# Down products of two row groups by Strassen's scheme on slab pairs, in a spectral filter with a gated FFN

## The chip, the cores and the metric

The kernel runs on one core of one Trainium2 chip. The metric is the device time of one execution in microseconds (us); for the kernel before, the median of three runs is 199.85 us (199.35 to 199.93).

A core has five engines, each with an instruction queue of its own that runs in order: PE (TensorE, matmuls; PEld is its loading of weights), DVE (VectorE), ACT (ScalarE), POOL (GpSimd) and SP (SyncE, which here only issues DMAs). They wait for each other through semaphores. Matmuls write to PSUM, from where DVE and ACT take the results.

## The reference

```python
x = A_x                                  # 1 x 2048 x 640, bf16
xn = _layernorm(x, axis=-1)
X = rfft2(xn) * (w_r + 1j * w_i)         # over rows (2048) and columns (640)
s = irfft2(X)
g = silu((gelu(xn @ w_gate) * (xn @ w_up)) @ w_down)   # 640 -> 1536 -> 640
return x + s * g
```

Two branches read the same normalised rows: a 2-D Fourier filter (s), and a gated feed-forward network (g). The product of the two is added to x.

## The kernel before

The 2048 rows are cut into 16 slabs of 128 rows, and the slabs into four groups of four (512 rows). Everything stays in SBUF, apart from two turns through DRAM in the Fourier branch (ZDR after the transform along columns, UDR after the filter).

**The order is written out by hand.** A list `back` holds the work of the FFN in 144 steps, and a list `plan` of the same length holds what is put behind each step with `put(step, function, ...)`. At the end a loop emits step 0, then its extras, step 1, and so on. Every engine runs its instructions in this order of emission; no scheduler moves any of them. A step number is therefore a place in the queue of each engine, not a time.

The steps: 0 to 23 belong to the gate and up products of group 0, 24 to 35 to its down product. Group 1 has steps 36 to 59 for gate and up and 60 to 71 for down; group 2 has 72 to 95 and 96 to 107; group 3 has 108 to 131 and 132 to 143.

**The FFN.** In `ffn_half(g, t, k)` five matmuls of 512 columns make one of the twelve 128-wide pieces t of the gate product (k = 0, bank psg) or of the up product (k = 1, bank psu) for 512 rows. ACT takes the gate out with gelu (`ge`, L807), DVE multiplies the up product by it (L809) into `uT[t]`, which lies transposed: the inner dimension on the partitions, rows along the free axis. `down_third(g, j, q)` then makes a third of the down product of slab j: per slab two halves of 320 columns, each a chain of twelve matmuls over t (L828), so 24 matmuls per slab and 96 per group. When a half is complete, the gate of the output is formed: silu by ACT for groups 0 and 3, and for groups 1 and 2 a tanh on ACT (L836) and a multiply-add on DVE (L837). The banks psg and psu have two buffers each.

**The rows.** `slab_T(n, 2)` transposes a normalised slab by a DMA transpose on SP's queue (L539) into `xnT`, the moving operand of gate and up. For slabs 8 to 11 it is put at steps 34, 37, 40, 43; for slabs 12 to 15 at steps 65, 68, 71, 74.

**The Fourier branch.** For each slab `slab_S1` (five small matmuls) and `slab_D` (six) transform the folded rows: ACT copies the result to a tile `zd` (L591, six buffers), and SP stores it in two DMAs to ZDR (L594). The last is slab 15's `slab_D`, put at step 60. At the same step `load_B2` issues ten DMAs that read ZDR back the other way round into B2 (L612); they wait for the stores. Then come eleven bursts: `s2_in` (matmuls px, L638; copy by ACT, L646; two multiplications with the filter's weights on DVE, L650) and `s2_out` (matmuls pu, L665; copies by ACT, L671; a store to UDR on SP, L674). The first `s2_in` is put at step 67. `load_V` at step 91 reads UDR back (Vin and W2), `gather` picks columns on DVE, and from step 99 the inverse transform runs along the columns (`slab_S1i`, `group_Di`), is combined (`group_cs`, `group_Y`), multiplied by the gate and added to x (`finish`, L778, L779), and stored.

**Where things lie.** X (16 slabs) is normalised in place. Its first 13 slabs later hold the bursts' products and the staging for UDR; after that all of it becomes Y, the result. The pool `xg` has five buffers for the `xnT` and the gates G of the groups. `uT` has one buffer.

The loop that emits everything:

```python
for s, b in enumerate(back):
    b[0](*b[1:])
    for it in plan[s]:
        it[0](*it[1:])
```

Of the kernel before, what the change touches and what calls it, by code (L numbers as in the profile page):

```python
# [14 lines left out]
P = 128  # L15
# [16 lines left out]
@with_exitstack  # L32
def kernel(
    ctx: ExitStack,
    tc: tile.TileContext,
    A_x: bass.AP,
    A_w_r: bass.AP,
    A_w_i: bass.AP,
    B_x: bass.AP,
    B_w_gate: bass.AP,  # L40
    B_w_up: bass.AP,
    B_w_down: bass.AP,
    out: bass.AP,
):

    nc = tc.nc
    x2 = A_x[0]
    xv = x2.rearrange("(n2 n1) d -> n2 n1 d", n1=NS)  # L50
    outv = out[0].rearrange("(n2 n1) d -> n1 n2 d", n1=NS)

    consts = ctx.enter_context(tc.tile_pool(name="consts", bufs=1))
    big = ctx.enter_context(tc.tile_pool(name="big", bufs=1))
    wts = ctx.enter_context(tc.tile_pool(name="wts", bufs=1))
    xg = ctx.enter_context(tc.tile_pool(name="xg", bufs=5))
    work = ctx.enter_context(tc.tile_pool(name="work", bufs=2))
    psA = ctx.enter_context(tc.tile_pool(name="psA", bufs=2, space=bass.MemoryType.PSUM))
    psB = ctx.enter_context(tc.tile_pool(name="psB", bufs=2, space=bass.MemoryType.PSUM))
    dram = ctx.enter_context(tc.tile_pool(name="dscratch", bufs=1, space=bass.MemoryType.DRAM))  # L60

    ZDR = dram.tile([2, 2, NS, 64, L], BF16)
    UDR = dram.tile([2, 2, NS, 64, L], BF16)


    X = big.tile([P, NS, D], BF16, tag="sX")
    Wg = wts.tile([P, 5, F], BF16)
    Wu = wts.tile([P, 5, F], BF16)
    Wd = wts.tile([P, NT, D], BF16)
    W1 = wts.tile([P, 2, NS, L], BF16)  # L70
    W2 = wts.tile([P, 2, NS, L], BF16)
    wgv = B_w_gate.rearrange("(c p) f -> p c f", p=P)
    wuv = B_w_up.rearrange("(c p) f -> p c f", p=P)
    with tc.manual_schedule():
        build(nc, locals())


def build(nc, env):
    consts, big, wts, xg, work, psA, psB = (env[k] for k in ("consts", "big", "wts", "xg", "work", "psA", "psB"))
# [58 lines left out]
    Tfwd = consts.tile([P, NS, P], BF16)  # L138
    FT = consts.tile([P, 5, TW], BF16)
# [337 lines left out]
    def fold_y(n0, n, k):  # L477
        xn = slabs(n0, n)
        t = scratch(n0, 2304, n, 256)
        if k == 0:  # L480
            nc.vector.tensor_tensor(out=t, in0=xn[:, :, 0:256], in1=xn[:, :, 256:512], op=ALU.add)
            return
        if k == 1:
            y = work.tile([P, 4, P], BF16, tag="y0", bufs=2, name="y0")
            for a in range(n):
                y0s[n0 + a] = y[:, a, :]
            y0s[n0, n] = y = y[:, 0:n, :]
            nc.vector.tensor_tensor(out=y, in0=t[:, :, 0:P], in1=t[:, :, P:256], op=ALU.add)
            return
        y = y0s[n0, n]  # L490
        nc.vector.tensor_tensor(out=y, in0=y, in1=xn[:, :, 512:640], op=ALU.add)
# [26 lines left out]
    def fold_b(n0, n, k):  # L518
        if k == 0:
            f = work.tile([P, 4, 512], BF16, tag="xf", bufs=2, name="f")  # L520
            for a in range(n):
                xf[n0 + a] = f[:, a, :]
            xf[n0, n] = f[:, 0:n, :]
        s4 = scratch(n0, 1280, n, 512).rearrange("p s (w d) -> p s w d", w=2)
        dm = xf[n0, n].rearrange("p k (g d) -> p k g d", g=4)
        gs, op = ((slice(0, 4, 3), ALU.add), (slice(1, 3), ALU.subtract))[k]
        nc.vector.tensor_tensor(out=dm[:, :, gs, :], in0=s4[:, :, :, 0:P], in1=s4[:, :, :, 255:127:-1], op=op)
# [4 lines left out]
    def slab_T(n1, eng):  # L532
        assert ("n", n1) in done
        g, j = n1 // 4, n1 % 4
        if g not in xnT:
            xnT[g] = xg.tile([P, 5, 512], BF16, tag="xg", name=f"xnT{g}")
# [45 lines left out]
    def slab_D(n1):  # L582
# [7 lines left out]
        zd = work.tile([P, 2, 330], BF16, tag="zd", bufs=6, name="zd")  # L590
# [15 lines left out]
    def load_B2():  # L606
# [7 lines left out]
        sc = X[:, 0:13, :].rearrange("p n d -> p (n d)")  # L614
        n_u, n_p = 2 * 3 * L, 2 * 3 * WB
        st_b["p"] = sc[:, 0:4 * n_p].rearrange("p (s q k x) -> p s q k x", s=2, q=2, k=2)
        st_b["u"] = sc[:, 4 * n_p:4 * n_p + 2 * n_u].rearrange("p (s k x) -> p s k x", s=2, k=2)
# [64 lines left out]
    def load_V():  # L682
        Va = big.tile([P, VA, 2 * L], BF16, tag="sB", name="Vin")
# [8 lines left out]
        st_c["Y"] = big.tile([P, NS, D], BF16, tag="sX", name="Yall")  # L692
# [13 lines left out]
    def load_xt(pair):  # L706
        t = work.tile([P, 4, 512], BF16, tag="xf", bufs=2, name="xt")
        t = t.rearrange("p a b -> p (a b)")[:, 0:2 * D].rearrange("p (a d) -> p a d", a=2)
# [45 lines left out]
    def group_Y(i, q):  # L754
        n0, n = DG[i]
        cs = quad(csbuf, i)
        Y = st_c["Y"][:, n0:n0 + n, :].rearrange("p a (h n) -> p a h n", h=2)
# [13 lines left out]
    def finish(n1):  # L771
# [5 lines left out]
        Y = st_c["Y"][:, n1, sl]  # L777
# [5 lines left out]
    uT = {}  # L783

    def bank(k):
        return psA.tile([P, 512], FP32, tag="gu"[k], name="ps" + "gu"[k])

    def new_uT(g):
        if g not in uT:
            uT[g] = work.tile([P, NT, 512], BF16, tag="uT", bufs=1, name=f"uT{g}")  # L790
# [5 lines left out]
    def ffn_piece(g, t, k, c0, c1_):  # L796
        new_uT(g)
# [4 lines left out]
        for c in range(5):  # L802
            nc.tensor.matmul(ps, lhsT=WT[:, c, t * P:(t + 1) * P], rhs=xnT[g][:, c, c0:c1_],  # L803
                             start=(c == 0), stop=(c == 4))
        if k == 0:
            ges[t] = work.tile([P, 512], BF16, tag="ge", bufs=3, name="ge")[:, c0:c1_]
            nc.scalar.activation(out=ges[t], in_=ps, func=ACT.Gelu_apprx_tanh)  # L807
        else:
            nc.vector.tensor_tensor(out=uT[g][:, t, c0:c1_], in0=ps, in1=ges[t], op=ALU.mult)  # L809
# [7 lines left out]

    def down_third(g, j, q):
        if j == 0 and q == 0:
            Gt[g] = xg.tile([P, 4, D], BF16, tag="xg", name=f"G{g}")  # L820
        m = (len(cut(4 * g + j)) - 1) * NT // 3
        for i in range(m * q, m * q + m):
# [5 lines left out]
            nc.tensor.matmul(ph, lhsT=uT[g][:, t, j * P:(j + 1) * P], rhs=Wd[:, t, c0:c1_],  # L828
                             start=(t == 0), stop=(t == NT - 1))
            if t == NT - 1:  # L830
                Gk = Gt[g][:, j, c0:c1_]
                if g in BY_SILU:
                    nc.scalar.activation(out=Gk, in_=ph, func=ACT.Silu)  # L833
                else:
                    th = work.tile([P, 320], FP32, tag="th", bufs=2)
                    nc.scalar.activation(out=th, in_=ph, func=ACT.Tanh, scale=0.5)  # L836
                    nc.vector.scalar_tensor_tensor(out=Gk, in0=th, scalar=1.0, in1=ph, op0=ALU.add, op1=ALU.mult)  # L837
                Gok.add((4 * g + j, k))
                finish(4 * g + j)
# [17 lines left out]
    def slab_Tparts(n1):  # L857
        if n1 == 0:
            xnT[0] = xg.tile([P, 5, 512], BF16, tag="xg", name="xnT0")
# [7 lines left out]
    NP = 8  # L867
    back = [(run, (ffn_slab, 0, GG), (norm_parts, 1), (slab_Tparts, 1), (vt_iota, 1), (ffn_slab, 0, UU),
# [7 lines left out]
    for g in range(4):  # L876
        for t in range(NP if g == 0 else 0, NT):
            for k in range(2):
                back.append((ffn_half, g, t, k))
        for j in range(4):  # L880
# [46 lines left out]
    for at, *items in (  # L927
# [14 lines left out]
        for it in items:  # L942
            put(at, *it)
    F0 = 30
# [6 lines left out]
    for k in range(4):  # L951
        put(34 + 3 * k, slab_T, 8 + k, 2)
        put(65 + 3 * k, slab_T, 12 + k, 2)
# [12 lines left out]
    sb = z_end + 7  # L966
    for b in range(len(BURSTS)):
        put(sb + 24 * b // 11, s2_in, b)
        if b > 0:
            put(sb + 24 * b // 11, s2_out, b - 1)  # L970
    put(sb + 23, s2_out, len(BURSTS) - 1)
    sb += 24
# [6 lines left out]
    for i, (n0, n) in enumerate(DG):  # L979
        a = vs0 + 7 * i  # L980
        for k in range(n):
            put(a + (2 * k if n == 3 else 1), slab_S1i, n0 + k)
# [56 lines left out]
```

## Time and profile before

| | |
|---|---|
| Median of three runs | 199.85 us |
| Profiled execution, first to last instruction (span) | 197.8 us |
| Granted PE clock, mean over the span | 1.000 |
| PE busy | 193.1 us |
| DVE busy | 131.1 us |
| ACT busy | 124.3 us |
| POOL busy | 39.9 us, all before 75 us |
| Down matmuls of 128x320 (372 of 396) | mean 299 ns from start to result |
| Gate and up matmuls of 128x512 (400 of 580) | mean 379 ns from start to result |
| Group 1 down stage | 81.7 to 97.7 us |
| Group 2 down stage | 130.9 to 146.5 us |
| DMA issues for zd to ZDR | 32, of 80.2 KB, 2.8 us to landing |
| DMA transposes into xnT | 12, 2.9 us to landing |

Times in the profile count from the first instruction of the profiled execution. "SPq" rows are instructions of SP's queue that issue DMAs; their length is the time that the issue holds the queue, not the transfer. In a row of the chain "DMA ZDR<-zd" the length runs from the issue to the landing. "Idle before <-releaser" at the end of a row is how long the engine had waited and for whom.

### The profile page before, as it was taken

The page shows a single profiled execution, that of the slowest core. Times are in us where ns is not written, and L with a number is a line of the kernel's source. Part 1 is how long each engine was busy: PE and PEld are TensorE (multiplying, and loading weights), DVE is VectorE, ACT ScalarE, POOL GpSimd, SP SyncE. Part 2 cuts the span into 40 slices and gives each one's busy share as a digit, 9 for nine tenths or more (in the row PEclk, how much of TensorE's full clock was granted, in tenths as well). Part 3 has the DMA queues.
Part 4 walks back from the last instruction along what each step waited for, and adds up shares of the span by engine and source line. Part 5 has one row for each costly group of instructions (what it writes and reads, how often), then busy time and mean ns, then how long its engine had stood idle before and what let it go on. Part 6 is the DMA issues. An engine that isn't in the chain of part 4 may idle for free.

```text
span 197.8 us, 4159 instructions
## 1 busy us (share of the span) xinstructions
PE 193.1 (98%) x1541; PEld 119.0 (60%) x1541; DVE 131.1 (66%) x314; ACT 124.3 (63%) x219; POOL 39.9 (20%) x68
## 2 busy tenths in 40 slices
PE   7999999999999999999999999999999999999993
PEld 5798844777555555675534343467765555556773
DVE  7887888989899822124666555333349786978673
ACT  4668567866877666724878688524474738376632
POOL 4448588997310200000000000000000000000000
DMA  6999999768665783429952022359800416142522
GB/s 173 298 332 364 365 314 180 134 82 312 153 157 147 151 309 86 127 64 324 273 162 103 22 79 103 133 138 292 237 0 33 138 37 195 36 133 43 192 65 71
DMA packets 39509, 32.44 MB, mean 164 GB/s; under 512 B 13248, under 2 KB 38464, under 8 KB 39232
## 3 DMA queue, kind: packets, MB, share of 16 engines
q1 hardware_dynamic: 37424, 29.87, 53.8%
q10 hardware_dynamic: 1968, 0.98, 1.8%
q0 software_dynamic: 96, 1.31, 1.7%
q8 instruction: 12, 0.20, 0.4%
q14 instruction: 9, 0.07, 0.1%
HBM read 19.03 MB, written 7.88 MB: 136 GB/s over the span
## 4 chain that ended last, share of the span: by engine, by line
PE 90%; DMA 5%; DVE 2%; ACT 1%; issue 0%; SPq 0%
PE psg L803 27%; PE psu L803 26%; PE psg L828 11%; PE psu L828 11%; PE pv L720 2%; DMA ZDR<-zd 2%; PE pd L565 2%; PE pu L665 2%; PE pz L555 2%; PE px L638 2%; PE pd L586 2%; DMA B<-ZDR 2%; DMA X<-in_A_x_dram 1%; PE pd L569 1%; DVE st L180 1%; PE pt L863 1%
## 5 line engine op out<-in xcount | busy, mean ns | idle before, releaser
L803 PE MATMUL psg<-xnT,Wg 128*128 128x512 bf16 (+2 forms) x290 | 61.2, 342 | 0.0
L803 PE MATMUL psu<-xnT,Wu 128*128 128x512 bf16 (+2 forms) x290 | 61.1, 343 | 0.0
L809 DVE TENSOR_TENSOR uT<-psu,ge 128x512 bf16<-128x512 f32 (+2 forms) x58 | 34.4, 594 | 25.8 <-PE psu L803 23.6
L828 PEld LDWEIGHTS <-uT 128*128 128x128 bf16 x396 | 37.2, 98 | 14.1 <-issue 0.4
L807 ACT ACTIVATE ge<-psg 128x512 bf16<-128x512 f32 (+2 forms) x58 | 30.4, 523 | 22.3 <-PE psg L803 21.6
L803 PEld LDWEIGHTS <-Wu 128*128 128x128 bf16 x290 | 26.7, 98 | 23.5 <-issue 2.2
L803 PEld LDWEIGHTS <-Wg 128*128 128x128 bf16 x290 | 26.4, 98 | 20.5 <-issue 1.6
L828 PE MATMUL psg<-Wd,uT 128*128 128x320 bf16 (+1 forms) x204 | 30.5, 294 | 0.0
L828 PE MATMUL psu<-Wd,uT 128*128 128x320 bf16 (+1 forms) x192 | 28.9, 296 | 0.0
L650 DVE TENSOR_TENSOR X<-xs,W 128x972 bf16<-128x972 bf16 (+2 forms) x22 | 13.3, 648 | 10.7 <-ACT xs L646 10.7
L591 ACT CAST zd<-pd 128x660 bf16<-128x660 f32 x16 | 11.3, 706 | 9.8 <-PE pd L588 9.1
L722 ACT CAST W<-pv 128x640 bf16<-128x640 f32 x16 | 11.1, 696 | 5.0 <-PE pv L720 5.0
L180 DVE BATCH_NORM_STATS2 st<-X 128x6 f32<-128x320 bf16 x32 | 14.0, 476 | 0.4 <-DMA X<-in_A_x_dram 0.4
L745 ACT ACTIVATE W<-pd 128x960 bf16<-128x960 f32 (+2 forms) x14 | 10.1, 780 | 5.6 <-PE pd L569 5.5
L671 ACT CAST X<-pu 128x486 bf16<-128x486 f32 (+4 forms) x22 | 12.3, 558 | 0.3
L646 ACT CAST xs<-px 128x972 bf16<-128x972 f32 (+2 forms) x11 | 10.3, 937 | 3.4 <-PE px L638 3.4
L837 DVE SCALAR_TENSOR_TENSOR G<-th,psg 128x320 bf16<-128x320 f32 x8 | 3.9, 487 | 11.7 <-ACT th L836 11.7
L557 ACT CAST GEN<-pz 128x640 bf16<-128x640 f32 x16 | 11.2, 698 | 0.0
L751 DVE TENSOR_TENSOR W<-W 128x960 bf16<-128x960 bf16 (+1 forms) x12 | 6.9, 599 | 3.9 <-ACT W L745 3.8
L778 DVE TENSOR_TENSOR Yall<-Yall,G 128x640 bf16<-128x640 bf16 (+3 forms) x19 | 8.3, 435 | 1.6 <-ACT G L833 1.3
L779 DVE TENSOR_TENSOR Yall<-Yall,xt 128x640 bf16<-128x640 bf16 (+3 forms) x19 | 8.3, 439 | 0.7
L837 DVE SCALAR_TENSOR_TENSOR G<-th,psu 128x320 bf16<-128x320 f32 x8 | 3.9, 486 | 6.1 <-ACT th L836 6.1
(143 smaller groups left out, 213.9 us busy)
## 6 DMA issues: line engine op xcount, KB each, us to landing
ZDR<-zd SPq DMA_DIRECT2D x32, 80.2 KB, 2.8
UDR<-X SPq DMA_DIRECT2D x10, 240.8 KB, 2.4
xt<-in_A_x_dram SPq DMA_DIRECT2D x14, 160.0 KB, 3.0
out_dram<-Yall SPq DMA_DIRECT2D x14, 160.0 KB, 2.2
B<-ZDR SPq DMA_DIRECT2D x8, 240.8 KB, 4.2
W<-UDR SPq DMA_DIRECT2D x4, 481.5 KB, 6.7
X<-in_A_x_dram SPq DMA_DIRECT2D x3, 640.0 KB, 10.5
Wd<-in_B_w_down_dram SPq DMA_DIRECT2D x1, 1920.0 KB, 14.5
```

The lines of the kernel that those rows point to most:

```text
L180: nc.vector.bn_stats(out=st_n[n1][:, k, :], in_=X[:, n1, 320 * k:320 * k + 320])
L557: nc.scalar.copy(out=Zt[n1], in_=pz)
L591: nc.scalar.copy(out=zd.rearrange("p c (q e) -> p c q e", e=10), in_=pd[:, :, 0:330].rearrange("p c (e q) -> p c q e", q=33))
L646: nc.scalar.copy(out=xs, in_=px[:, :, 0:n * w].rearrange("p k (h l) -> p k h l", l=w))
L650: nc.vector.tensor_tensor(out=pp[-1], in0=xs, in1=WT[:, :, h0:h0 + n, l0:l0 + w], op=ALU.mult)
L671: nc.scalar.copy(out=us[:, :, :, c0:c0 + (w + 1 - m) // 2], in_=pv[:, :, :, m:w:2])
L722: nc.scalar.copy(out=vs, in_=pv)
L745: nc.scalar.activation(out=eo[:, b, :, a0:a1].rearrange("p k a n -> p a k n"), in_=py[b][:, a0:a1], func=ACT.Copy, scale=(2.0 if silu[a0] ...
L803: nc.tensor.matmul(ps, lhsT=WT[:, c, t * P:(t + 1) * P], rhs=xnT[g][:, c, c0:c1_], start=(c == 0), stop=(c == 4))
L807: nc.scalar.activation(out=ges[t], in_=ps, func=ACT.Gelu_apprx_tanh)
L809: nc.vector.tensor_tensor(out=uT[g][:, t, c0:c1_], in0=ps, in1=ges[t], op=ALU.mult)
L828: nc.tensor.matmul(ph, lhsT=uT[g][:, t, j * P:(j + 1) * P], rhs=Wd[:, t, c0:c1_], start=(t == 0), stop=(t == NT - 1))
```

## The change

Strassen's scheme (in Winograd's form) makes the product of two 2x2 block matrices with seven block products in place of eight, at the cost of sums of blocks before and after. It is used for the down product of groups 1 and 2.

- A group's four slabs make two pairs (a = 0, 1). One pair's rows are the two row blocks (slab j = 0, 1 of the pair); the inner dimension is cut into even and odd t (k = 0, 1; six pieces each), and the 640 columns into two halves (h). The block A(j, k) is 128 rows by 768, the block B(k, h) 768 by 320.
- `product(g, a, i)` makes block product i of 7: six matmuls of 320 columns in one bank. A group has 14 products, laid on its twelve down steps as 1, 1, 1, 1, 1, 2 and again.
- `w_sum`: the four sums of weight blocks, once, on DVE at steps 51, 52, 54 and 56. They lie in the first twelve slabs of X (`TS`).
- `u_sum`: the four sums of A blocks of a pair, each in two parts (t below 3 and above). One of the four is written in place into UT. Pair 0's others lie in the first XG slot, pair 1's in X slabs 12 to 15 (`SB`). Group 1: on DVE at step 52 (pair 0, first part), 57 (pair 1, first part), 59 (pair 0, second part); pair 1's second part one by one behind products 1 to 4 of pair 0. Group 2: the first parts on POOL at steps 84 and 87, the rest on DVE as in group 1 (pair 0's second part at step 95).
- The results are joined in six f32 tiles (`snf`): per pair two copies by ACT, five adds out of PSUM on DVE, two adds on POOL. The tanh and the multiply-add of the gate now read these tiles, and are put off: the tanh by one product, the multiply-add by two (`put_off`, `flush`).
- The transposes of slabs 12 to 15 (`slab_T`) go to steps 47, 50, 53, 56, since X slabs 12 to 15 are overwritten from step 57 on.
- The first burst goes to step 68; the bursts' steps follow the list `AT` and end at the same step as before. The first `slab_S1i` of each three slabs goes one step later.
- Buffers get fixed places: XG (five slots for xnT and G), UT, RX (folded rows, then UDR staging, then the loads of x), RZ (zd, then the bursts' products), RT (Tfwd, FT and y0, then the six f32 tiles). The first twelve slabs of Y lie behind Vin, the last four in X.

```diff
+    XG = consts.tile([P, 5, 5 * 512], BF16, name="XG")
+    UT = consts.tile([P, NT, 512], BF16, name="UT")
+    RX = consts.tile([P, 2, 4 * 512], BF16, name="RX")
+    RZ = consts.tile([P, 6, 2 * 330], BF16, name="RZ")
+    RT = consts.tile([P, 12 * 320], BF16, name="RT")
...
+    TS = X[:, 0:12, :].rearrange("p n d -> p (n d)").rearrange("p (i t c) -> p i t c", i=4, c=320)
+    SB = X[:, 12:NS, :].rearrange("p n d -> p (n d)")
...
+    A4 = UT.rearrange("p (t k) (a j c) -> p t k a j c", k=2, a=2, c=P)
+    B4 = Wd.rearrange("p (t k) (h c) -> p t k h c", k=2, h=2)
+    SS = [b[:, 0:3 * 6 * P].rearrange("p (i t c) -> p i t c", i=3, c=P) for b in (XG[:, 0, :], SB)]
+    snf = RT[:, 0:12 * 320].bitcast(FP32).rearrange("p (i c) -> p i c", c=320)
...
+    def u_sum(eng, a, t0, t1, ks=(0, 1, 2, 3)):
+        S = SS[a]
+        A = lambda j, k: A4[:, t0:t1, k, a, j, :]
+        s1, s2, s4 = (S[:, i, t0:t1, :] for i in range(3))
+        for k in ks:
+            out, in0, in1, op = ((s1, A(1, 0), A(1, 1), ALU.add), (s2, s1, A(0, 0), ALU.subtract),
+                                 (A(1, 0), A(0, 0), A(1, 0), ALU.subtract), (s4, A(0, 1), s2, ALU.subtract))[k]
+            eng.tensor_tensor(out=out, in0=in0, in1=in1, op=op)
...
+    def product(g, a, i):
...
+        ps = bank((i + a) % 2)[:, 0:320]
+        for t in range(6):
+            nc.tensor.matmul(ps, lhsT=lhs[:, t, :], rhs=rhs[:, t, :], start=(t == 0), stop=(t == 5))
+        flush()
+        if a == 0 and i in (1, 2, 3, 4):
+            u_sum(nc.vector, 1, TB, 6, (i - 1,))
...
+        if g in STR:
+            for k in range(12):
+                back.append((run,) + tuple((product, g) + divmod(i, 7) for i in range(k * 7 // 6, (k + 1) * 7 // 6)))
+            continue
...
+    for i, at in enumerate((51, 52, 54, 56)):
+        put(at, w_sum, i)
+    put(52, u_sum, nc.vector, 0, 0, 3)
+    put(57, u_sum, nc.vector, 1, 0, 3)
+    put(59, u_sum, nc.vector, 0, 3, 6)
+    for a, at in ((0, 84), (1, 87)):
+        put(at, u_sum, nc.gpsimd, a, 0, 3)
+    put(95, u_sum, nc.vector, 0, 3, 6)
...
-        put(65 + 3 * k, slab_T, 12 + k, 2)
+        put(47 + 3 * k, slab_T, 12 + k, 2)
...
-    sb = z_end + 7
+    sb = z_end + 8
+    AT = (0, 3, 5, 7, 9, 11, 13, 15, 17, 19, 21)
     for b in range(len(BURSTS)):
-        put(sb + 24 * b // 11, s2_in, b)
+        put(sb + AT[b], s2_in, b)
...
-            put(a + (2 * k if n == 3 else 1), slab_S1i, n0 + k)
+            put(a + ((1, 2, 4)[k] if n == 3 else 1), slab_S1i, n0 + k)
```

## The prediction

> **What bounds the kernel now.** I read the page's first table, then the groups by form, then SP's own timeline, then the chain of waits between 78 and 98 us.
>
> ```profile
> PE 193.1 (98%) x1541; PEld 119.0 (60%) x1541; DVE 131.1 (66%) x314; ACT 124.3 (63%) x219; POOL 39.9 (20%) x68
> ...
> L828 PE MATMUL psg<-Wd,uT 128*128 128x320 bf16 x192 | 29.7, 299 | 0.0
> ```
>
> The end is set by the stream of instructions on PE, which waits for almost nothing. The 299 ns is latency; what a matmul costs the stream is its spacing, and the chain in order of time gives that: twelve down matmuls in 1.63 us, 0.136 us each.
>
> ```profile
> 33.87 1.63 PE psg L828 x12
> ...
> 84.66 2.54 DMA ZDR<-zd
> ...
> 87.96 3.30 DMA B<-ZDR
> 91.26 0.04 issue
> 91.30 0.40 PE px L638 x3
> ```
>
> These last lines show the one place where the stream is tied to something else. The last forward-Fourier store goes out at 84.66 and lands at 87.20; only then are the B loads issued; the second of them lands at 91.26, and the rest of the first px matmuls start at 91.30. PE had come to px at 90.80, so it already waits here, for half a microsecond.
>
> What feeds that chain is SP's queue, with one zd copy of ACT to set beside it:
>
> ```profile
> 65.17 0.71 ACT L591 CAST zd<-pd 128x660 bf16<-128x660 f32 x1 [0.79 <-PE pd L588]
> ```
> ```profile
> 66.13 1.22 SPq L539 DMA_TRANSPOSE xnT<-X  x1
> 67.45 1.26 SPq L594 DMA_DIRECT2D ZDR<-zd  x2
> 68.80 1.92 SPq L448 DMA_TRANSPOSE N<-MG  x1
> 70.82 2.67 SPq L448 DMA_TRANSPOSE N<-MJ  x1
> 73.58 11.68 SPq L594 DMA_DIRECT2D ZDR<-zd  x16
> 87.53 4.64 SPq L612 DMA_DIRECT2D B<-ZDR  x10
> 92.42 1.59 SPq L539 DMA_TRANSPOSE xnT<-X  x1
> ```
>
> The zd copy at 65.17 is slab 8's (the last two, slabs 14 and 15, come at 81.91 and 83.30, the others every 2.75 us). It ends at 65.88, yet its stores are issued at 73.58: SP is 7.7 us behind. A pair of stores costs SP 1.26 us and about 0.08 to the next. Eight pairs so make 8 x 1.26 + 7 x 0.08 = 10.6 of the 11.68 us; the missing 1.04 lies in one long issue near 74.2 (five issues from 74.23 take 4.28 us), and the last four take 2.62, so 0.1 us at most is waiting. SP catches up with ACT exactly at the last two slabs. It has no room before the B loads.
>
> **The change, part by part.**
>
> Matmuls: each pair of slabs does 7 products of 6 matmuls instead of 8; two pairs in two groups save 24, at 0.136 us 3.26 us. They stand so: 4 in group 1 before the first px (10 products, 60 matmuls, where 64 stood), 8 after it, 12 in group 2.
>
> Moved DMA transposes: the four of slabs 12 to 15 went from steps 65, 68, 71, 74 (behind the B loads, 92.42 and later) to 47, 50, 53, 56. On SP that is behind the stores of slabs 8, 9, 11 and 12, ahead of three more pairs and all ten B loads. Each costs 1.22 and 0.08 to the next, 1.30; four make 5.2. Less the 0.1 of waiting, the last store and the B loads come 5.1 us later. From both sides: a transpose's issue lies between 1.21 and 2.12 us (all twelve of xnT). Least shift, if the 1.04 too were room: 4 x 1.21 - 1.04 = 3.8. Most: 4 x 2.12 = 8.5; the long ones stood among the B loads, with much in flight, and the four before them, among zd stores as here, took 1.22 to 1.26. I take 5.1.
>
> The Trainium skill, "DMA: Bandwidth & Descriptors", section "Issuing engines are not separate DMA queues", says of the sequencer's time to start a DMA that it "is usually small relative to the DMA itself". Here a transpose issues for 1.22 us and lands after 2.6 to 2.9, so the trace does not agree; by that rule the four would cost nothing and the sum would be the first rival's.
>
> What PE makes of it: the B wait ended last before and ends last after, so px moves by the whole shift: from 91.30 to 96.4. PE would be there at 81.71 + 60 x 0.136 + 0.44 (slab 15's slab_D) = 90.3 if nothing else held it. The 4 matmuls saved ahead of px drown in the wait; the 20 after it count, 2.72 us. **Net: 5.1 - 2.7 = +2.4 us.**
>
> The in-place sums: the sums of pair 1 (u_sum at step 57) write over X slabs 12 to 14 and so wait for those transposes. Slab 14's is issued at 73.58 + 4 x 1.34 + 1.04 + 2 x 1.30 = 82.6 and lands 2.6 later, at 85.2. DVE stands there from about 82; queued behind it are the last uT multiply of group 1 (0.69) and pair 0's late sums, and the second product needs the first, the third product the others. PE so idles about 2.6 us in the second product (from 83.7 to 86.3) and comes to px near 93.1 with 3.3 us left to wait. This splits the idle time and adds none as long as 93.1 is under 96.4.
>
> Added DVE work in group 1's steps 51 to 59: four sums of weight blocks of 1920 elements (954 ns for 1536 and 688 for 1024: 1.15 us each by the slope) and eight slab sums of 384 (325 for 320, 422 for 512: 0.36 each), 7.5 us. It hides in this stretch:
>
> ```profile
> 68.85:81.70 12.85, 12.85 (x102) 7.43 (x101) 3.10 (x6) 9.14 (x15) 1.00 (x2) 1.00 0.55 182
> ```
>
> After the length stand PE, PEld, DVE, ACT and POOL: DVE is busy 3.10 of 12.85 us. If the cover were gone, a uT multiply would be late, and PE would notice only when it wants that psu bank again, two t later, some 5 us.
>
> Added work beside the products, per group: 10 DVE adds out of PSUM at 0.49 (the row of the gate's multiply), 8 slab sums at 0.36: 7.8 us; 4 ACT copies at 0.44; 4 POOL adds of 320, between 0.2 (a tensor operation of 4 elements) and 1.6 (660 elements, f32). In group 1 it lies inside PE's wait. In group 2's stage, 130.92 to 146.50, DVE is busy 4.67 and would come to 12.5 of 13.9 us. The point there is the third product: it needs the last multiply and two sums, 0.1 + 0.69 + 0.72 = 1.5 us after the last up matmul, and PE comes to it after 1.63. I take 0; at most 0.3 if each handover costs 0.1 more. Group 2's early sums on POOL (8 of 384 elements, at most 1.6 each, 12.8 us) have the eleven steps to 95, over 15 us. DVE's gather behind them waits for Vin, which landed at 133.82, 2.9 us after the stage's start; DVE comes to it at 4.
>
> Places without price: the products p now lie in RZ, written after B has landed; the staging u and the x loads in RX; Y in the old B2 space, written after its last reader. The bursts start a step later, end at the same step and issue the same DMAs. The first inverse matmuls of each three slabs (slab_S1i) go one step later in PE's own queue, with their five matmuls and one ACT copy; Vin has landed by then.
>
> Sum: 197.8 + 2.4 = 200.2 us of span. The median of the runs, 199.85, lies 2.05 above the span, so **202.3 us**.
>
> **Rivals.**
>
> 1. *The transposes are hidden* (faster). If SP's issues cost PE nothing, B lands as before and all 24 matmuls count: 199.85 - 3.3 = 196.6. The point is a shift of 2.72 us, 0.68 for a transpose. For it: DMA engines have room then (share 0.55). Against it: SP back to back from 66 to 85, and the issue rows. 0.15; another 0.07 for a shift between.
>
> 2. *The idle time also slows PE's clock.*
>
> ```profile
> 1.17 4.53 PE L602 MATMUL psg<-GEN 128*128 128x256 bf16 x21 [1.17 <-DVE eps L220]
> ```
>
> At the start 21 matmuls of 256 columns take 4.53 us, 0.21 each, while 512 columns later take 1.08 us for five, so 256 would take 0.108: after long idling PE runs at half pace for some 4 us, though the granted clock reads 1.00. The same behind px would cost 20 x 0.1 = 2 us: 204.3. Against it: the idle time comes in pieces, 2.6, 2.3 and 1.0 us, with matmuls between.
>
> The Trainium skill, "TensorE: Matmul & The Clock Gate", Part 1, puts the drop to half after an idle window of about 3.4 us. The head of the trace agrees with the half; how long an idle piece it takes no row here shows.
>
> With this go transposes of up to 2.12 us, 199.85 + 8.5 - 2.7 = 205.7. Together 0.16.
>
> 3. *DVE becomes the bound in group 2*: the 1.6 us gained there are lost, 203.9. Its 12.5 of 13.9 us speak against it; part of the 0.16.
>
> **How the numbers follow.** Forecast, 200.9 to 203.4: 0.62. Clock, longer transposes or DVE, up to 206: 0.16. Hidden transposes, near 196.6: 0.15. Between: 0.07. A measurement tells 0.3%, 0.6 us, from no change. Faster: 0.15 and half of the 0.07, 0.18; same 0.03; slower 0.79. The range 200.0 to 205.0 leaves out the hidden case and the far end, 0.2.
>
> **What would show it.** In the changed profile: four transposes between the ZDR stores from 75 us on, the last store issued near 89.8 and the first B load near 92.7; PE idle some 2.5 us near 84 (released by DVE) and some 3 us more ahead of px, which starts at 95.4 and goes on at 96.4; 42 down matmuls a pair at 0.136; no PE idle time in group 2. I am wrong if the first B load is issued by 89, or if PE waits for DVE in group 2.

## The result, and the profile after

| | median of the runs, us | profiled execution, us | its span, us | its granted clock |
|---|---|---|---|---|
| before | 199.6 (199.07 to 199.93) | 199.85 | 197.8 | 1.000 |
| after | 204.69 (202.96 to 205.68) | 205.68 | 203.5 | 0.992 |

The change makes the kernel slower: 1.0258 of the time before, 95% interval 1.0206 to 1.0309. (The ratios in this document are taken over undisturbed runs only, so one can differ a little from the quotient of two medians.)

First SP's timeline of the changed kernel, in the stretch that decided the prediction. The columns are start, length, engine and line, operation; on SP the length is the time that the issues hold the queue. L550 is a transpose, L605 the zd stores, L623 the loads of B.

```profile
77.38 1.24 SPq L550 DMA_TRANSPOSE XG<-X  x1
...
80.03 1.24 SPq L550 DMA_TRANSPOSE XG<-X  x1
...
84.02 1.24 SPq L550 DMA_TRANSPOSE XG<-X  x1
85.35 1.23 SPq L605 DMA_DIRECT2D ZDR<-RZ  x2
86.67 1.24 SPq L550 DMA_TRANSPOSE XG<-X  x1
88.01 3.89 SPq L605 DMA_DIRECT2D ZDR<-RZ  x6
93.44 4.82 SPq L623 DMA_DIRECT2D B<-ZDR  x10
```

The four transposes stand between the stores, and the first B load is issued at 93.44, where before it was 87.53: 5.9 us later.

The timeline of PE (L897 is a block product, L648 px; the bracket gives idle time and who ended it):

```profile
81.99 0.98 PE L897 MATMUL psg<-Wd,UT 128*128 128x320 bf16 x6
...
83.11 0.84 PE L897 MATMUL psu<-Wd,UT 128*128 128x320 bf16 x5
87.73 0.45 PE L897 MATMUL psu<-Wd,UT 128*128 128x320 bf16 x1 [3.78 <-DVE UT L814]
87.97 1.81 PE L897 MATMUL psg<-X,XG 128*128 128x320 bf16 x6
89.57 1.75 PE L897 MATMUL psu<-X,UT 128*128 128x320 bf16 x6
91.15 0.98 PE L897 MATMUL psg<-X,XG 128*128 128x320 bf16 x6
...
95.23 0.98 PE L897 MATMUL psu<-X 128*128 128x320 bf16 x6
96.32 0.91 PE L648 MATMUL px<-B,MG 64*64 64x162 bf16 x5
```

PE stops in the second product for 3.78 us. The products after it start 1.60 and 1.58 us apart, where six matmuls otherwise take 0.81: PE runs at half pace from 87.97 to 91.15, and then at full pace again. The granted clock says the same. In this row of the windows (length, busy time of PE, PEld, DVE, ACT and POOL, then granted clock, DMA share, GB/s) it is 0.50, and in the 3.8 us ahead of it 1.00:

```profile
87.71:91.12 3.41, 3.39 (x13) 1.94 (x14) 3.38 (x11) 0.47 (x1) 0.00 (x0) 0.50 0.49 120
```

PE reaches px when B has all but landed. Who held PE in the second product is on DVE's timeline (L878 is a slab sum, L814 the multiply for which PE waits):

```profile
82.73 0.36 DVE L878 TENSOR_TENSOR X<-X,UT 128x384 bf16<-128x384 bf16 x1 [2.37 <-DMA XG<-X]
83.00 0.35 DVE L878 TENSOR_TENSOR UT<-UT 128x384 bf16<-128x384 bf16 x1
86.71 0.36 DVE L878 TENSOR_TENSOR X<-UT,X 128x384 bf16<-128x384 bf16 x1 [3.36 <-DMA XG<-X]
86.99 0.68 DVE L814 TENSOR_TENSOR UT<-psu,ge 128x512 bf16<-128x512 f32 x1
```

Two sums wait for transposes (2.37 and 3.36 us) before they may write over X, and the multiply stands behind them.

The wait for the forward Fourier part is not all. The windows show the stretch above and the stage of the bursts behind it, first before, then after:

```profile
81.70:97.40 15.70, 15.59 (x139) 10.53 (x137) 6.46 (x12) 7.61 (x15) 0.00 (x0) 1.00 0.75 213
97.40:132.00 34.60, 34.60 (x243) 14.22 (x236) 19.14 (x31) 24.61 (x42) 0.00 (x0) 1.00 0.34 103
```
```profile
81.70:97.40 15.70, 11.66 (x80) 7.38 (x79) 8.75 (x23) 4.86 (x12) 2.14 (x3) 0.89 0.51 138
97.40:132.00 34.60, 33.73 (x254) 14.44 (x253) 26.11 (x38) 27.04 (x46) 11.13 (x10) 1.00 0.32 112
```

After, PE is idle for 4.0 us of the first window and 0.9 of the second; before, for 0.1 and for nothing. POOL's 11.13 us in the second row are new. Two rows of the groups by form, the filter multiplies of the bursts, say what they did (the number behind the comma is the mean of one in ns). First before, then after:

```profile
L650 DVE TENSOR_TENSOR X<-xs,W 128x972 bf16<-128x972 bf16 x10 | 6.2, 665 | 5.4 <-ACT xs L646 5.4
L650 DVE TENSOR_TENSOR X<-xs,W 128x954 bf16<-128x954 bf16 x10 | 6.2, 661 | 4.3 <-ACT xs L646 4.3
```
```profile
L660 DVE TENSOR_TENSOR RZ<-xs,W 128x972 bf16<-128x972 bf16 x10 | 8.3, 873 | 3.1 <-ACT xs L656 3.1
L660 DVE TENSOR_TENSOR RZ<-xs,W 128x954 bf16<-128x954 bf16 x10 | 7.9, 831 | 2.4 <-ACT xs L656 2.3
```

The last loss stands at group 2's products:

```profile
142.32 0.33 PE L731 MATMUL pv<-Tinv,VY 128*128 128x128 bf16 x3 [1.06 <-DMA VY<-UDR]
```

The first inverse matmuls wait 1.06 us for V. Its loads were issued at 136.95, as group 2's products began (136.97); before, they were issued at 128.83, 1.9 us ahead of that stage's first matmul (130.76).

The sum can be made from PE's records alone. The first px splits it: "from" is the start of the first matmul behind it, and all that follows is added up from start to start, in us. The idle time in front of a matmul counts as that matmul's; V is the idle time before the first inverse matmuls.

| | from | px | pu | V | all else | last matmul starts |
|---|---|---|---|---|---|---|
| before | 91.63 | 2.24 | 5.49 | 0 | 95.06 | 194.42 |
| after | 97.16 | 2.58 | 6.91 | 1.06 | 92.35 | 200.06 |
| e1 | 96.33 | 2.24 | 5.49 | 0 | 96.73 | 200.80 |
| e2 | 91.67 | 2.58 | 6.91 | 1.24 | 92.38 | 194.77 |
| e9 | 91.27 | 2.58 | 6.90 | 1.37 | 92.48 | 194.60 |
| e11 | 91.33 | 2.24 | 5.49 | 0 | 93.13 | 192.19 |
| e12 | 91.32 | 2.41 | 6.06 | 0.79 | 93.16 | 193.74 |

The first two rows: 5.53 us of shift, 1.76 at px and pu, 1.06 at V, less 2.71 of matmuls, make the 5.64 by which the ends differ. The other rows are the experiments of the next section.

### The profile page after: what moved, and what is told of

The parts are those of the page before. It is cut to its first block, busy times and chain, and to the rows that moved or that the text cites. A ratio compares the mean times of both kernels' runs of the same rounds, so it can differ in the third digit from the quotient of the medians.

```text
span 203.5 us, 4203 instructions
## 1 busy us (share of the span) xinstructions
PE 192.9 (95%) x1517; PEld 117.8 (58%) x1517; DVE 154.6 (76%) x362; ACT 127.5 (63%) x227; POOL 56.2 (28%) x84
## 4 chain that ended last, share of the span: by engine, by line
PE 83%; DMA 6%; DVE 4%; ACT 3%; SPq 1%; issue 1%; DVEq 0%; ACTq 0%
PE psg L807 24%; PE psu L807 24%; PE psg L938 6%; PE psu L938 5%; PE psu L897 3%; PE psg L897 3%; DVE RZ L660 3%; PE psg L613 2%; PE pv L731 2%; PE pz L566 2%; PE pd L576 2%; ACT xs L656 2%; PE pd L597 2%; PE pu L675 2%; DMA VY<-UDR 2%; DMA B<-ZDR 1%
## 5 line engine op out<-in xcount | busy, mean ns | idle before, releaser
L807 PE MATMUL psg<-XG,Wg 128*128 128x512 bf16 (+2 forms) x290 | 61.2, 343 | 0.0
L807 PE MATMUL psu<-XG,Wu 128*128 128x512 bf16 (+2 forms) x290 | 61.1, 342 | 0.0
L814 DVE TENSOR_TENSOR UT<-psu,ge 128x512 bf16<-128x512 f32 (+2 forms) x58 | 34.4, 593 | 17.9 <-PE psu L807 15.3
L938 PEld LDWEIGHTS <-UT 128*128 128x128 bf16 x204 | 19.0, 98 | 6.8
L660 DVE TENSOR_TENSOR RZ<-xs,W 128x972 bf16<-128x972 bf16 (+2 forms) x22 | 17.1, 820 | 5.7 <-ACT xs L656 5.7
L845 ACT ACTIVATE th<-RT 128x320 f32<-128x320 f32 x16 | 7.2, 468 | 16.2 <-DVE RT L902 15.5
L602 ACT CAST RZ<-pd 128x660 bf16<-128x660 f32 x16 | 11.3, 708 | 9.2 <-PE pd L599 9.1
L938 PE MATMUL psg<-Wd,UT 128*128 128x320 bf16 (+1 forms) x108 | 15.5, 290 | 0.0
L897 PEld LDWEIGHTS <-UT 128*128 128x128 bf16 x96 | 9.5, 101 | 8.3 <-DVE UT L814 4.1
L938 PE MATMUL psu<-Wd,UT 128*128 128x320 bf16 (+1 forms) x96 | 14.0, 292 | 0.0
L681 ACT CAST RX<-pu 128x486 bf16<-128x486 f32 (+4 forms) x22 | 12.2, 556 | 0.3
```

Source lines behind the costliest of these rows:

```text
L602: nc.scalar.copy(out=zd.rearrange("p c (q e) -> p c q e", e=10), in_=pd[:, :, 0:330].rearrange("p c (e q) -> p c q e", q=33))
L660: nc.vector.tensor_tensor(out=pp[-1], in0=xs, in1=WT[:, :, h0:h0 + n, l0:l0 + w], op=ALU.mult)
L681: nc.scalar.copy(out=us[:, :, :, c0:c0 + (w + 1 - m) // 2], in_=pv[:, :, :, m:w:2])
L814: nc.vector.tensor_tensor(out=UT[:, t, c0:c1_], in0=ps, in1=ges[t], op=ALU.mult)
L897: nc.tensor.matmul(ps, lhsT=lhs[:, t, :], rhs=rhs[:, t, :], start=(t == 0), stop=(t == 5))
L938: nc.tensor.matmul(ph, lhsT=UT[:, t, j * P:(j + 1) * P], rhs=Wd[:, t, c0:c1_], start=(t == 0), stop=(t == NT - 1))
```

## The experiments

The median of the kernel before was 199.25 to 199.29 beside all of these. A kernel's time is compared with that.

| run | median, us | ratio to before | 95% interval |
|---|---|---|---|
| e1 move alone | 206.19 | 1.0342 | 1.0297 to 1.0388 |
| e2 second weight on POOL's queue | 200.3 | 1.0052 | 1.0027 to 1.0078 |
| e3 transposes on PE | 201.32 | 1.0087 | 1.0058 to 1.0117 |
| e4 group 2 alone | 198.69 | 0.9967 | 0.9951 to 0.9982 |
| e5 = e2, sums on DVE | 199.9 | 1.0026 | 1.0003 to 1.0050 |
| e6 = e5, second burst later | 200.03 | 1.0017 | 0.9993 to 1.0041 |
| e7 = e5, bursts even | 200.08 | 1.0033 | 1.0013 to 1.0053 |
| e8 before, second weight on POOL's queue | 199.3 | 1.0002 | 0.9991 to 1.0012 |
| e9 transposes back, alone | 199.25 | 0.9998 | 0.9980 to 1.0015 |
| e10 all mended | 198.82 | 0.9970 | 0.9954 to 0.9986 |
| e11 = e4, sums on DVE | 197.36 | 0.9900 | 0.9883 to 0.9916 |
| e12 = e11 and group 1 | 198.85 | 0.9985 | 0.9961 to 1.0010 |

### The move of the transposes alone (e1)

The kernel before, with the one line of the move:

```diff
-        put(65 + 3 * k, slab_T, 12 + k, 2)
+        put(47 + 3 * k, slab_T, 12 + k, 2)
```

> The kernel before with one edit: the four DMA transposes of slabs 12 to 15 at steps 47, 50, 53, 56 in place of 65 to 74. No Strassen product in it. Theory (SP's queue has no room, each transpose costs 1.3 us there, px waits for B): the first B load is issued 5 to 6 us later than 87.5, so near 93, PE idles 5 to 6 us ahead of px and nowhere else, and the time is 204.5 to 206, slower than the changed kernel or equal to it. If PE's clock falls in that one piece of idle time, up to 2 us more. Rival (issues are hidden, the loss of the changed kernel comes from its sums): 199.3 to 200.2, as before.

It took 206.19 us, so the move alone costs 6.9, more than the whole change. The first B load is issued at 92.56, as the theory said; PE idles 4.2 us ahead of px, less than the 5 to 6 expected. PE's timeline of this run (L638 is px, L828 a down matmul):

```profile
90.69 0.71 PE L828 MATMUL psu<-Wd,uT 128*128 128x320 bf16 x4
95.41 0.36 PE L638 MATMUL px<-B,MG 64*64 64x162 bf16 x2 [4.01 <-DMA B<-ZDR]
96.00 0.40 PE L638 MATMUL px<-B,MG 64*64 64x486 bf16 x3 [0.23 <-DMA B<-ZDR]
96.33 2.05 PE L828 MATMUL psu<-Wd,uT 128*128 128x320 bf16 x8
98.18 2.18 PE L828 MATMUL psg<-Wd,uT 128*128 128x320 bf16 x8
```

The wait is nearly in one piece here, and the matmuls that slow down stand behind px: the first eight start in 1.85 us, the next in 2.11, where 8 x 0.136 is 1.09. The granted clock is 1.00 while PE waits and in the first 1.2 us behind the wait, and then falls for 3.4 us:

```profile
96.64:100.06 3.42, 3.42 (x16) 1.92 (x13) 1.73 (x3) 1.21 (x2) 0.00 (x0) 0.50 1.02 365
```

The row of e1 in the table has the whole of it: 4.70 us of shift, and 1.67 more in "all else". In the changed kernel the slow matmuls ran inside the wait for B and cost next to nothing.

### What else relieves SP's queue (e2), or replaces the transposes (e3)

e2 is the changed kernel with nine loads of the second filter weight issued from POOL's queue (one of four such lines):

```diff
-        nc.sync.dma_start(out=WT[p0:p0 + 61:4, lo].rearrange("p h l -> p (h l)"),
+        (nc.sync, nc.gpsimd)[i].dma_start(out=WT[p0:p0 + 61:4, lo].rearrange("p h l -> p (h l)"),
```

> The changed kernel with the nine loads of the second filter weight issued from POOL's queue instead of SP's, at the same steps. That takes 9 x 0.65 = 5.9 us off SP ahead of the B loads, against 5.3 us for the four transposes. Theory: the first B load is issued by 88.5, DVE's wait for slab 14's transpose and PE's idle time in the second product go, and the time is 196.3 to 198. Rival 1 (the sums on DVE and POOL are the loss): stays at 202 or more. Rival 2 (the transposes slow the DMA engines, not SP's queue): B loads stay late by 3 us or more, time above 200.

SP is then ahead, and the transposes fit in. SP's timeline of this run:

```profile
82.36 3.88 SPq L605 DMA_DIRECT2D ZDR<-RZ  x6
87.90 4.65 SPq L623 DMA_DIRECT2D B<-ZDR  x10
```

The first B load is back at 87.90 and the gap in the second product is gone. The queue was the cause of both. But the time is 200.3 and not 196.3 to 198. Its row of the table: from px on it starts where the kernel before starts (91.67), and the 2.68 us of matmuls go again at px and pu (1.76) and V (1.24). That half of the expectation failed, and e4 to e7 and e9 to e12 go after it.

e3 leaves the four slabs at their early steps but transposes them on PE:

```diff
-        put(47 + 3 * k, slab_T, 12 + k, 2)
+        put(47 + 3 * k, slab_T, 12 + k, 1)
```

> The changed kernel with the four transposes of slabs 12 to 15 made by PE (five small transposes each, copied by ACT) at the same steps 47 to 56 instead of by DMA. Theory: SP is as in the kernel before, px waits half a microsecond as before; the 3.3 us of matmuls are gained less 4 x 0.28 = 1.1 us for PE's transposes: 197 to 199. Rival (sums are the loss): 202 or more.

201.32 us. The B loads come at 89.55. The transposes took PE 1.1 us more (1.22 to 2.33), and twice PE stood 0.52 us for ACT, which copied zd. The 5 us of the queue went, and about 2 us came back as work of PE and ACT ahead of B: the expectation failed by that.

### The control: SP relieved in the kernel before (e8)

> The kernel before with the second filter weight's loads off SP's queue, nothing else. Theory: in the kernel before SP was late by about as much as PE was; B lands earlier by up to 5 us but PE comes to px at 90.8 and gains its half microsecond of wait at most: 198.7 to 199.3, ratio 0.995 to 1.0. Rival (SP's lateness costs the kernel before elsewhere, in its transposes of slabs 12 to 15): 197.5 to 198.5, and then part of what w_on_pool gained is not the change's.

199.3 us, ratio 1.0002, the upper end of the theory's range. Relief of SP is worth nothing to the kernel before; what it gained in e2 was the change's own loss.

### Which part of the change gains: group 2 alone (e4), and its sums on DVE (e11)

e4 is the changed kernel with seven products in group 2 alone; group 1, the transposes and the bursts are as before (the lines for group 1's sums and the bursts' steps are left out here):

```diff
-    STR = (1, 2)
+    STR = (2,)
...
-        put(47 + 3 * k, slab_T, 12 + k, 2)
+        put(65 + 3 * k, slab_T, 12 + k, 2)
```

> Strassen's products in group 2 alone; group 1, the bursts' steps and the transposes (65 to 74) as in the kernel before, buffers in their new places. Twelve matmuls fewer, 1.6 us. Theory: no shift of B; the weight sums hide; 197.8 to 199 where group 2's wait for Vin (1.1 us in the changed kernel) and DVE's slow multiplications beside POOL's sums (0.5 us) give back at most 1.2 of it. Rival (DVE is the bound in group 2): no gain or a loss, 199.6 or more.

198.69 us, faster than before by 0.3% and in the theory's range, so the products work where nothing has to be moved for them. PE had two gaps left: 0.66 at 120.0 (pu, behind a filter multiply of DVE beside POOL's sums) and 0.57 at 136.4 (the first inverse matmuls, behind DVE's gather). The timelines of DVE and POOL in the changed kernel show the same meeting:

```profile
117.91 1.25 DVE L660 TENSOR_TENSOR RZ<-xs,W 128x972 bf16<-128x972 bf16 x2 [0.58 <-ACT xs L656]
...
123.04 0.68 DVE L814 TENSOR_TENSOR UT<-psu,ge 128x512 bf16<-128x512 f32 x1
123.91 2.66 DVE L660 TENSOR_TENSOR RZ<-xs,W 128x972 bf16<-128x972 bf16 x2 [0.19 <-ACT xs L656]
```
```profile
120.41 0.91 POOL L878 TENSOR_TENSOR XG<-UT 128x384 bf16<-128x384 bf16 x1 [18.41 <-DVE UT L814]
...
123.85 0.91 POOL L878 TENSOR_TENSOR XG<-UT,XG 128x384 bf16<-128x384 bf16 x1
124.72 1.33 POOL L878 TENSOR_TENSOR X<-UT 128x384 bf16<-128x384 bf16 x1
```

Two multiplies take 1.25 us before POOL starts its sums, and 2.66 beside them. The multiply L814, with one input in PSUM, stays at 0.68 in the same stretch. e11 moves the early sums:

```diff
-        put(at, u_sum, nc.gpsimd, a, 0, 3)
+        put(at, u_sum, nc.vector, a, 0, 3)
```

> The kernel with the seven products in group 2 alone (g2_only, 198.69) with the early sums on DVE instead of POOL. Theory: the gap of 0.66 us at 120 (pu behind the doubled filter multiply) goes: 197.8 to 198.3. Rival: DVE, busier by 2.9 us, is late elsewhere: 198.5 to 199.2.

197.36 us, better than the theory's range and outside e4's interval. Its groups by form:

```profile
L660 DVE TENSOR_TENSOR RZ<-xs,W 128x972 bf16<-128x972 bf16 x10 | 6.2, 664 | 3.8 <-ACT xs L656 2.8 <-DMA B<-ZDR 1.0
L660 DVE TENSOR_TENSOR RZ<-xs,W 128x954 bf16<-128x954 bf16 x10 | 6.2, 660 | 4.3 <-ACT xs L656 4.3
```

The multiplies are as fast as before though DVE has 8 x 0.36 us more to do, and both gaps of e4 are gone. From start to start they were 0.85 and 0.73 us longer than the same places in e11, 1.59 of the 1.66 us by which the last matmuls of the two profiles differ (193.85 and 192.19; the medians differ by 1.33). No idle time of PE above 0.06 us stands behind 7 us in this profile. It beats both kernels.

### The same sums in the whole change, and the steps of the bursts (e5, e6, e7)

e5 is e2 with the line of e11.

> The changed kernel with the second filter weight's loads off SP's queue (as in w_on_pool), and the early slab sums of group 2 (steps 84 and 87, eight of 384 elements) on DVE instead of POOL. Theory: the filter multiplies of the bursts double (0.66 to 1.33 us) because POOL's sums run beside them; with the sums on DVE the multiplies between 117 and 128 us go back to 0.66 us, the PE gaps of 0.11 and 0.26 us ahead of pu there go away, and the time falls by 0.3 to 0.6 us against w_on_pool: 199.7 to 200.0. Rival (the multiplies are slow for another reason, for instance where their inputs lie): they stay at 1.33 us and DVE, with 8 x 0.36 us more to do, makes it slower: 200.3 to 201.

e6 and e7 are e5 with other steps for the bursts:

```diff
-    AT = (0, 3, 5, 7, 9, 11, 13, 15, 17, 19, 21)
+    AT = (0, 4, 6, 8, 10, 11, 13, 15, 17, 18, 20)
```
```diff
-    AT = (0, 3, 5, 7, 9, 11, 13, 15, 17, 19, 21)
+    AT = (0, 2, 4, 6, 8, 10, 12, 14, 16, 18, 20)
```

> sums_on_dve with the bursts at offsets 0, 4, 6, 8, 10, 11, 13, 15, 17, 18, 20 in place of 0, 3, 5, 7, 9, 11, 13, 15, 17, 19, 21: the first bursts clear of the products' copies, the last ones' stores at the steps of the kernel before. Theory (the crowding of the bursts behind the products and the later last stores cost the gain): the pu gaps of 0.2 and 0.3 us after the first two bursts shrink, UDR lands a step earlier, and the wait of the first inverse matmuls for V (1.2 us) goes: 197.5 to 198.7. Rival (the bursts' excess comes from DVE and ACT being full, wherever they stand): within 0.5 us of sums_on_dve.

> sums_on_dve with the bursts evenly at every second step (0, 2, ... 20), so that the second stands amid the products of group 1. Theory of crowding behind the products: the first bursts wait longer for ACT and DVE, which the products' copies and adds hold (0.5 to 1.5 us more in pu), while the end is as early as in second_burst_later: 198.0 to 199.5. Rival (the number of steps does not matter): as sums_on_dve, 199.5 to 200.

In e5 the multiplies of 954 elements are back at 660 ns and the two pu gaps near 120 us are gone, so the mechanism holds; the time, 199.9, lies in the expected range, but its interval overlaps e2's, so the gain by itself is not shown here (e4 against e11 shows it).

e6 and e7 took 200.03 and 200.08: the theories of the steps failed, and the rivals held (e7 is 0.08 above its range). The profiles show where the time goes, though each is of one of the shorter executions of its kernel (199.05, 198.65 and 199.21). The gaps of PE from px on, by what they wait for, in us:

| | B at px | pu for ACT or DVE | inverse matmuls for V or the gather | sum |
|---|---|---|---|---|
| e5 | 0.66 + 0.16 | 0.20 + 0.30 | 0.52 | 1.84 |
| e6 | 0.35 + 0.16 | 0.63 + 0.35 + 0.21 | none | 1.70 |
| e7 | 0.44 + 0.16 | 0.74 + 0.39 | 0.20 + 0.25 | 2.18 |

e6 removes the wait for V, as expected, and pays for it at pu. Moving the bursts moves the loss.

### The move undone alone (e9), and everything mended (e10)

e9 is the changed kernel with the transposes put back. Group 1's second pair can keep its sums in the slot of xnT3, which is empty until the transposes of slabs 12 to 15 fill it. X is then not written over, and the transposes may stand behind the B loads:

```diff
-    SS = [b[:, 0:3 * 6 * P].rearrange("p (i t c) -> p i t c", i=3, c=P) for b in (XG[:, 0, :], SB)]
+    SS = [b[:, 0:3 * 6 * P].rearrange("p (i t c) -> p i t c", i=3, c=P) for b in (XG[:, 0, :], XG[:, 3, :], SB)]
...
-        S = SS[a]
+        S = SS[a * g]
...
-        put(47 + 3 * k, slab_T, 12 + k, 2)
+        put(72 + 3 * k, slab_T, 12 + k, 2)
```

> The changed kernel with one thing undone: the four DMA transposes of slabs 12 to 15 stand behind the B loads again (steps 72 to 81), which is possible because group 1's sums of the second pair lie in the slot of xnT3 instead of X. Theory (the shift of SP's queue costs 5.5 us, the saved matmuls behind px give 2.7, the bursts lose 1.8 and the wait for V 0 to 1.25): the first B load is issued at 87 to 88.5 again, PE has no gap in the second product, and the time is 198.4 to 199.8, 5 to 6 us under the changed kernel. Rival (a second cause of the loss lies in the products themselves, for instance DVE's work or the clock): 200.5 to 203.

199.25 us, in the theory's range: 5.4 us less than the changed kernel by the transposes' place (and the slot of the sums that allows it), or 5.1 where each is compared with the kernel before beside it (199.6 and 199.26). SP's timeline of e9:

```profile
73.38 11.91 SPq L605 DMA_DIRECT2D ZDR<-RZ  x16
87.34 4.79 SPq L623 DMA_DIRECT2D B<-ZDR  x10
93.78 1.23 SPq L550 DMA_TRANSPOSE XG<-X  x1
```

The B loads are where they were, and PE has no gap in the products ahead of px. Its row of the table is e2's but for a few tenths: what is saved behind px is lost at pu and V.

e10 takes the other losses away too (e9 with e2's, e5's and e6's edits).

> transposes_back with the three other losses taken away too: the second filter weight's loads off SP's queue, group 2's early sums on DVE, the bursts' steps of second_burst_later. Theory: B lands before PE comes to px, so the four matmuls ahead of px count too, and the first inverse matmuls don't wait: 199.25 - 3.3 + about 1.2 left in the bursts, 196.8 to 197.8. Rival (PE at px is bound by something else that comes late, as DVE's or ACT's copies, so that the gain is lost there again): 198.5 to 199.5.

198.82 us: a miss of 1 us, in the rival's range. Its profile still has 0.63 + 0.35 + 0.21 us at pu (for ACT's copies) and 0.54 at the gather. And SP, though free, cannot go early:

```profile
70.98 14.57 SPq L605 DMA_DIRECT2D ZDR<-RZ  x16
87.55 4.67 SPq L623 DMA_DIRECT2D B<-ZDR  x10
```

The sixteen stores now spread over 14.57 us where back to back they took 11.68: SP waits for zd. The last copy of zd by ACT starts at 83.40 in this run (83.30 before), and so the first B load is at 87.55 as ever. ACT is not the one that binds either: that copy starts 0.05 us after PE has ended slab 15's `slab_D` (83.34; before, 83.26 and 0.04). So the place of this `slab_D` in PE's own order, step 60, holds B as firmly as SP's queue did, and taking SP away moves B not at all. No run puts the `slab_D` earlier.

### What group 1's products are worth (e12)

e12 is the best kernel, e11, with group 1's seven products added, and nothing moved but the transposes to steps 72 to 81, the sums' place as in e9.

> The best kernel so far (g2_sums_on_dve: seven products in group 2 alone, 197.36) with the seven products in group 1 too, the bursts at the steps of the kernel before, the sums of group 1's second pair in xnT3's slot and the transposes of slabs 12 to 15 at steps 72 to 81. It tells what group 1's products are worth with all else equal. Theory (B is bound by ACT's last zd copy at 83 and lands at 91.3 at the earliest, so four of the twelve saved matmuls drown in the wait, and DVE and ACT, full with the products' adds and copies from 82 to 97, put off the first bursts): 196.8 to 198.5, the saved 1.6 us mostly given back. Rival (only the bursts' other steps cost it in all_mended): 195.8 to 196.6.

198.85 us, 1.5 more than e11 with 12 matmuls less, and 0.35 above the theory's range: the saving is not "mostly" but more than given back. PE's timeline:

```profile
88.47 0.98 PE L897 MATMUL psg<-Wd,UT 128*128 128x320 bf16 x6
90.46 0.37 PE L648 MATMUL px<-B,MG 64*64 64x162 bf16 x2 [1.02 <-DMA B<-ZDR]
90.99 0.40 PE L648 MATMUL px<-B,MG 64*64 64x486 bf16 x3 [0.16 <-DMA B<-ZDR]
91.32 0.99 PE L897 MATMUL psu<-X,XG 128*128 128x320 bf16 x6
...
93.29 0.84 PE L675 MATMUL pu<-RZ,N 64*64 64x162 bf16 x10
```

The work behind px starts at 91.32; in e11 it starts at 91.33. Behind it stand 5 products, 30 matmuls, where e11 has 32. So ten of the twelve saved matmuls went into the wait for B, and the two that count, 0.27 us, are not to be seen in "all else" (93.16 against 93.13). The bursts then lose 0.74 at px and pu and 0.79 at V, nearly all of the 1.55 between the two ends.

## Why the prediction was right, and where it was off

- **The queue.** The step that carried the forecast held: the four transposes held SP for 1.24 us each, 1.33 to the next issue, and e9 gives 5.4 us back by their place (5.1 against the kernel before beside it), against 5.1 forecast; in e1 the move alone shifts px by 4.70. In the changed kernel the first B load came 5.9 us later and px 5.53. That this lies so near 5.1 is partly luck, since two things that the forecast left out nearly cancel. SP's stores at 65.97 answer to those at 64.31 before, so it was 1.66 us late ahead of the moved transposes, with an issue of 1.70 us for a weight load (such a load otherwise takes 0.61). In e1 the same stores are 0.83 us late and the first B load 5.03: a queue that is full until B hands its lateness on. Against it, the last store, 6.6 us later than before (91.30, forecast 89.8), landed in 2.06 us and not 2.54, and the first B load followed its landing in 0.08 and not 0.33.
- **PE's gap by way of DVE.** Forecast 2.6 us from 83.7 to 86.3; it was 3.78 from 83.9 to 87.7, since slab 14's transpose was issued at 84.02 and not at 82.6. The path (transpose, sum, multiply behind it, second product) is what the DVE rows show.
- **Rival 2, the clock.** I held against it that the idle time comes in pieces. One piece was long enough: behind 3.78 us six matmuls took 1.60, at a granted clock of 0.50 for 3.41 us. It cost nothing to speak of because PE then reached px as B landed (0.12 and 0.14 us of wait left); in e1, behind 4.01 us and with no wait left, it cost 1.67 us, within the 2 of the rival's price. The Trainium skill, "TensorE: Matmul & The Clock Gate", Part 1, has the drop after an idle window of about 3.4 us; by that rule these two gaps should slow PE, and those of up to 1.37 us in e2 and e9 should not, and the traces agree. The gap itself was forecast too short (2.6 us) to meet it. Three of the four runs of the changed kernel had a clock of 0.989 to 0.992, the fourth 0.999 and 202.96 us; whether the missing dip is why that one was shorter is open, as no trace of it exists. (The 1.00 that the prediction read at the head of the trace is no reading: the kernel before has no clock record at all, and in the changed kernel's trace the first stands at 5.79 us.)
- **The matmuls.** 24 fewer at 0.136, and the four ahead of px drowned in the wait, as said. e12 shows the same in a sharper form, ten of twelve.
- **"Places without price."** This step was mis-sized: px and pu took 1.76 us more. From start to start all of it lies at five places: 0.40 and 0.52 at the third and the fourth px with the pu behind them, where pu waits for ACT's copies of the pu before it (L681; e6 and e7 show that other steps don't free it); 0.31 and 0.45 at the two pu that wait for a filter multiply beside POOL's sums (gone in e5); and 0.09 at the last pu. The idle times in brackets (0.20, 0.30, 0.11 and 0.25) show only half of that, since a matmul's row runs on to its result, 0.30 us for a spacing of 0.136, and covers the first part of a wait.
- **Group 2 at nothing.** By its own sign ("or if PE waits for DVE in group 2") the prediction was wrong here: pu waits 0.11 and 0.25 us for filter multiplies there. I priced POOL's sums by their own length (at most 1.6; measured 0.91 to 1.33) and found them hidden, and they were. What I left out is what they do to DVE: 0.66 to 1.33 for the filter multiplies beside them. The Trainium skill, "SBUF — State Buffer", "Summary: rules for kernel authors", says of a DVE operation with two SBUF inputs and a GpSimd operation that reads SBUF that the second to issue is blocked until the first finishes. The rows agree as far as they go: L660 has both inputs in SBUF and doubles, L814 has one in PSUM and stays at 0.68. Whether one waits out the other or both go at half pace, rows of 1.33 on both engines don't tell.
- **"Vin has landed by then."** Wrong by 1.06 us. The V loads follow the last store's landing, and from the last copy's end to their issue passed 4.3 us (132.64 to 136.95) where it had been 2.4 (126.43 to 128.83). The traffic of the DMA engines from the issue of the first of the last four stores to the landing of the last, in 40 slices, shows a hole; first before, then after:

```profile
GB/s 0 0 0 0 0 0 0 91 310 401 419 328 401 456 328 383 401 364 328 364 92 0 0 0 0 0 0 121 316 280 61 30 225 291 201 31 0 0 0 0
```
```profile
GB/s 0 0 0 0 0 0 302 454 317 403 288 389 403 317 374 317 15 0 0 14 14 0 14 14 29 19 259 283 101 106 322 212 24 24 19 66 0 0 0 0
q8 instruction: 1, 0.02, 1.9%
```

After, a load of instructions (queue q8, one packet of 16 KB, 1.59 us from 132.40) falls into the transfer, and the stores' held packets go on at 133.97, as it ends. In all eight runs with a long landing (the first of these stores took 2.4 to 4.4 us, the second 4.1 to 4.7) such a load stands in that transfer; in the other six (before, e1, e3, e4, e8, e11: 2.0 to 2.1 and 2.4 to 2.8 us) it was over at most 0.15 us after the first of the four stores was issued. It is the eighth of twelve, and comes after 1947 to 1978 recorded matmuls and weight loads in every run. With 12 matmuls fewer in group 1 it so falls later against the bursts; e3, which adds 20 transposes on PE, is back in time. No run moves the load alone, so this cause is argued from the traces, not tested. e6, with the last stores at the steps of before, has no wait for V in spite of the long landing; e12, with all bursts there, still has one.
- **The size of the miss.** The forecast span was 200.2, the measured one 203.5: 0.43 of shift beyond 5.1, 1.76 at px and pu and 1.06 at V make 3.25 of the 3.3. The median, 204.69, is only 2.4 above the forecast of 202.3, since the profiled execution is the longest of its four. Luck had a part in this: the two terms put at nothing, 2.8 us, are more than the whole net forecast of +2.4, and the time stayed under 205.0 because that bound had room for a slower clock and longer transposes.

## What to carry to other kernels

A saved instruction counts only behind the last wait that another chain sets: find the waits that don't depend on the engine you relieve, and count what lies between the last of them and the end. What frees a buffer for the saving (here an earlier transpose) is paid on its own queue; look first for a place that nothing has to be moved for. And an operation that is hidden by its own length may still slow the engine beside it, so the price of "unused" POOL time is read from DVE's rows. Idle time in the profile understates what a wait costs PE; add up from start to start.

## What the runs showed of the hardware that was not expected

- DVE's multiply of two bf16 inputs in SBUF (128 x 972) takes 0.66 us alone and 1.33 beside POOL's tensor operations, and POOL's sums go from 0.91 to 1.33. DVE's multiply with an input in PSUM is not touched. Taking the sums off POOL gave 1.3 us (e4 to e11), though DVE got 2.9 us more work.
- PE runs at half pace for 3.4 us (granted clock 0.50) behind an idle time of 3.8 to 4.0 us, in the middle of a kernel whose PE had hardly paused for 70 us: six matmuls of 320 columns in 1.60 us for 0.81, 1.67 us lost in all in e1. In the changed kernel the drop comes as the idle time ends, in e1 1.2 us later.
- A load of 16 KB of instructions takes 0.9 to 1.8 us on the DMA queues around this place, and stores that are in flight beside it land in 4.1 to 4.7 us where they otherwise take 2.4 to 2.8.
